# Decode attention on one core: all small PSUM tiles in one bank, a third V granule kept in PSUM

## The chip, the core and the metric

The kernel runs on one core of a Trainium2 chip. The metric is the device time in microseconds (us) of one execution; lower is better. TensorE is written PE, its weight loads PEld, VectorE DVE, ScalarE ACT, GpSimd POOL and SyncE SP, as in the profile.

## The reference

Two decoder layers with the same weights and the same caches run on eight rows (B) of one token each. D is 640, there are 32 heads of 128, 4096 cached positions, and a feed-forward width of 1728. All data are bf16.

```python
def A(x, k_cache, v_cache, wq, wo):      # x: (8, 1, 640)
    q = (x @ wq).reshape(B, Sq, 32, 128).transpose(0, 2, 1, 3)
    scores = einsum("bhqd,bhkd->bhqk", q, k) * 128 ** -0.5
    p = softmax(scores, axis=-1)
    o = einsum("bhqk,bhkd->bhqd", p, v)
    return o.transpose(0, 2, 1, 3).reshape(B, Sq, 4096) @ wo
def F(x, w1, w2):
    return relu(x @ w1) @ w2

x = x + A(layernorm(x));  x = x + F(layernorm(x))
x = x + A(layernorm(x));  x = x + F(layernorm(x))
```

Both layers read the same K and V caches, so what of a row's cache still lies on the chip when its second layer comes needs no second load.

## The kernel before, in words

**Tiles.** Heads go in pairs; a pair has one K tile and one V tile of 2 MB. Each tile is four granules of 512 KiB (128 partitions of 2048 bf16). An arena in SBUF has 26 slots (`G`) of one granule each. A *visit* is one head pair of one row in one layer: 16 pairs, 8 rows, 2 layers, so 256 visits.

**Order.** A planner in Python, `plan`, writes out the order of all work for all engines ahead of time, and nothing reorders it later. Row 0 runs its first layer. Then, for each row b, four visits of row b+1's first layer (`AHEAD`) stand before row b's second layer, so that the feed-forward steps of row b's first layer have time to finish. The second layer takes pairs 15, 14, 13 first, and then 0 to 12. K of visit i stands before V of visit i-1.

**What stays on the chip.** The granules that the second layer needs first are kept in the arena: 21 granules (`G - SPARE`), K of pairs 15, 14, 13, V of 15 and 14, and the first of V of pair 13. While they are kept, five slots rotate. The next `STASH` granules, of V of pair 13, are copied into PSUM when the first layer has used them (`stash`, L464 to L470, two VectorE copies each) and back into the arena for the second layer (`unstash`, L472 to L475, one copy on ScalarE and one on VectorE each). These granules are not loaded a second time. PSUM has eight banks; a stashed granule takes two.

**Loads.** SP issues every load (`do_load`, L478), in the planner's order, when the slots that it fills are free. The planner puts up to several neighbouring granules into one load (`LEADS`) where many slots are free; while granules are kept, loads are single.

**Steps of a visit**, with the lines of the profile:

- K granules (L524): 16 weight loads and matmuls each, scores into `s_ps`.
- `M1` (L530): VectorE takes the maximum of the scores per partition. `T` (L534): TensorE turns it into `blk_ps`. `M2` (L538, L540): VectorE takes the maximum over that. `B` (L543): TensorE broadcasts it into `blk_ps`. `E` (L547, L551): ScalarE reads it and takes two exponentials from `s_ps`.
- `L` (L556): TensorE sums the exponentials over partitions into `blk_ps`. `I` (L562, L566): VectorE reduces and inverts.
- V granules (L512): four matmuls each into `o_ps`. `OC` (L570): ScalarE copies the result out.
- `OG` (L575): TensorE gathers it into `oy_ps`. `O` (L585): VectorE reads that and scales it.
- First layer, and the last row's second layer: `W` (L592), TensorE, the output projection into `oy_ps`; `Y` (L601), VectorE, adds it to x.
- Second layer: `Q` (L496), TensorE, the query of a later pair into `blk_ps`; `QC` (L504), ScalarE, copies it out.

At a row's end in the first layer come the steps of `finish`: sums, `mean` (L355) and `var` (L369) by TensorE into `oy_ps` with VectorE reading each (L359, L390), an inverse square root on GpSimd (L391 to L401, L375), five `up` steps (L417) and a relu (L425, L428), five `down` steps (L434) and an `add` (L441), and then the same normalisation again for the second layer's queries. The planner deals these steps out between the granules, one or two after each.

**PSUM banks before:** `o_ps`, `s_ps`, `blk_ps` and `oy_ps` have one bank each, and four hold the two stashed granules. `s_ps` has two halves, for even and odd visits:

```python
s_tiles[i] = s_ps[:, i % 2]
```

Of the kernel before, what the change touches and what calls it, by code (L numbers as in the profile page):

```python
# [9 lines left out]
FP32 = mybir.dt.float32  # L10
BF16 = mybir.dt.bfloat16
ACT = mybir.ActivationFunctionType
ALU = mybir.AluOpType
# [4 lines left out]
GP = 4  # L18
G = 26
SPARE = 5  # L20
STASH = 2
LEADS = ((9, 8), (6, 4), (5, 2))
AHEAD = 4
BANK = 512
# [215 lines left out]
def kernel(  # L240
# [91 lines left out]
    arena = kv.tile([P, G * GW], BF16, name="arena")  # L332
    OR = 96 + CJ
    o_ps = ps.tile([P, CJ * Dh], FP32, name="o_ps")
    s_ps = ps.tile([P, 2, 2 * NJ], FP32, name="s_ps")
    blk_ps = ps.tile([P, BANK], FP32, name="blk_ps")
    oy_ps = ps.tile([P, BANK], FP32, name="oy_ps")
    stash_ps = [ps.tile([P, 2 * BANK], BF16, name=f"stash{n}_ps") for n in range(STASH * GW // (2 * BANK))]
    per = len(stash_ps) // STASH
    nc.vector.memset(o_ps, 0.0)  # L340

    up_parts = [range(f, min(f + 3, FC)) for f in range(0, FC, 3)]
    visits, ops = plan(B, NP, len(up_parts), DC)
    q1, s_tiles, P_tiles, m_tiles, o_tiles, blk, oy, invL, oT, nmax, st = ({} for _ in range(11))

    def ln_steps(b0, nb, xln, key):
        x = xT[:, b0 : b0 + nb, :]

        def sums():
            s1 = st[key, "s1"] = sm.tile([P, nb], FP32, name="s1", bufs=1)  # L350
            nc.vector.tensor_reduce(out=s1, in_=x, axis=AX.X, op=ALU.add)

        def mean():
            st[key, "mean"] = oy_ps[:, 64 : 64 + nb]
            nc.tensor.matmul(st[key, "mean"], lhsT=ones_f, rhs=st[key, "s1"], start=True, stop=True)  # L355

        def center():
            xc = st[key, "xc"] = sm.tile([P, nb, DC], FP32, name="xc", bufs=1)
            nc.vector.scalar_tensor_tensor(  # L359
                out=xc, in0=_free(st[key, "mean"], [(1, nb), (0, DC)]), scalar=-1.0 / D, in1=x, op0=ALU.mult, op1=ALU.add  # L360
            )
            sq = sm.tile([P, nb, DC], FP32, name="sq", bufs=1)
            nc.vector.tensor_tensor(out=sq, in0=xc, in1=xc, op=ALU.mult)
            s2 = st[key, "s2"] = sm.tile([P, nb], FP32, name="s2", bufs=1)
            nc.vector.tensor_reduce(out=s2, in_=sq, axis=AX.X, op=ALU.add)

        def var():
            st[key, "var"] = oy_ps[:, 72 : 72 + nb]
# [35 lines left out]
    def finish_steps(layer, b):  # L404


        b0, nb = (b, 1) if layer == 0 else (0, B)
        xf = sm.tile([P, nb, DC], BF16, name="xf", bufs=1)
        key = layer, b

        def up(k):
            if k == 0:
                st[key, "h"] = oy_ps[:, 128 : 128 + FC * nb].rearrange("p (f b) -> p f b", b=nb)
            for f in up_parts[k]:
                fs = f_sizes[f]
                for c in range(DC):
                    nc.tensor.matmul(  # L417
                        st[key, "h"][:fs, f, :], lhsT=w1_sb[:, c, f * P : f * P + fs], rhs=xf[:, :, c],
                        start=(c == 0), stop=(c == DC - 1),
                    )  # L420

        def relu():
            hT = st[key, "hT"] = sm.tile([P, FC, nb], BF16, name="hT", bufs=1)
            if n_full:
                nc.scalar.activation(out=hT[:, :n_full], in_=st[key, "h"][:, :n_full], func=ACT.Relu)  # L425
            if Dff % P:
                rem = Dff % P
                nc.scalar.activation(out=hT[:rem, n_full:], in_=st[key, "h"][:rem, n_full:], func=ACT.Relu)  # L428

        def down(c):  # L430
            if c == 0:
                st[key, "y"] = oy_ps[:, 256 : 256 + DC * nb].rearrange("p (c b) -> p c b", b=nb)
            for f, fs in enumerate(f_sizes):
                nc.tensor.matmul(  # L434
                    st[key, "y"][:, c, :], lhsT=w2_sb[:fs, f, c * P : (c + 1) * P],
                    rhs=st[key, "hT"][:fs, f, :], start=(f == 0), stop=(f == FC - 1),
                )
# [12 lines left out]
        return first, ln_steps(b, 1, xlns[b], (key, 2))  # L450
# [28 lines left out]

    def do_q0(g):  # L480

        q_ps = blk_ps[:, 256 : 256 + 2 * GP * B].rearrange("p (h b) -> p h b", b=B)
        for h in range(2 * GP):
            for c in range(DC):
                nc.tensor.matmul(
                    q_ps[:, h, :], lhsT=wq_sb[:, g, c, h * Dh : (h + 1) * Dh], rhs=xln0[:, :, c],
                    start=(c == 0), stop=(c == DC - 1),
                )
        nc.scalar.copy(out=q0[:, g * 2 * GP : (g + 1) * 2 * GP, :], in_=q_ps)

    def do_q(b, hp):
        q_ps = st["q", b, hp] = blk_ps[:, 320:322]
        g, n = divmod(hp, GP)
        for h in range(2):
            for c in range(DC):
                nc.tensor.matmul(  # L496
                    q_ps[:, h : h + 1], lhsT=wq_sb[:, g, c, (2 * n + h) * Dh : (2 * n + h + 1) * Dh],
                    rhs=xlns[b][:, 0, c : c + 1], start=(c == 0), stop=(c == DC - 1),
                )

    def take_q(b, hp):
        if b not in q1:
            q1[b] = sm.tile([P, H], BF16, name="q1", bufs=2)
        nc.scalar.copy(out=q1[b][:, 2 * hp : 2 * hp + 2], in_=st.pop(("q", b, hp)))  # L504

    def do_mm(which, i, g, u):
        layer, b, hp = visits[i]
# [22 lines left out]
        nc.vector.tensor_reduce(out=m_tiles[i], in_=s_tiles[i].rearrange("p (h j) -> p h j", h=2), axis=AX.X, op=ALU.max)  # L530

    def do_t(i):
        blk[i] = blk_ps[:, : P + 2 + 2 * NJ]
        nc.tensor.matmul(blk[i][:2, :P], lhsT=m_tiles.pop(i), rhs=ident, start=True, stop=True)  # L534

    def do_m2(i):
        hmx = sm.tile([2, 1], FP32, name="hmx")
        nc.vector.tensor_reduce(out=hmx, in_=blk[i][:2, :P], axis=AX.X, op=ALU.max)  # L538
        nmax[i] = sm.tile([2, 2], BF16, name="diag")
        nc.vector.tensor_tensor(out=nmax[i], in0=ident[:2, :2], in1=_free(hmx, [(0, 2)]), op=ALU.mult)  # L540

    def do_b(i):
        nc.tensor.matmul(blk[i][:, P : P + 2], lhsT=ones_b, rhs=nmax.pop(i), start=True, stop=True)  # L543

    def do_e(i):
        nm = sm.tile([P, 2], FP32, name="nmax")
        nc.scalar.activation(out=nm, in_=blk[i][:, P : P + 2], func=ACT.Copy, scale=-inv_sqrt_dh)  # L547
# [6 lines left out]

    def do_l(i):
        nc.tensor.matmul(  # L556
            blk[i][:, P + 2 :], lhsT=ones_p, rhs=P_tiles[i].rearrange("p h j -> p (h j)"), start=True, stop=True
        )

    def do_i(i):  # L560
        L = sm.tile([P, 2], FP32, name="lsum")
        nc.vector.tensor_reduce(  # L562
            out=L, in_=blk.pop(i)[:, P + 2 :].rearrange("p (h j) -> p h j", h=2), axis=AX.X, op=ALU.add
        )
        invL[i] = sm.tile([P, 2], FP32, name="invL", bufs=3)
        nc.vector.reciprocal(out=invL[i], in_=L)  # L566
# [3 lines left out]
        nc.scalar.copy(out=o_tiles[i][:OR], in_=o_ps[:OR, :].rearrange("p (j d) -> p j d", j=CJ))  # L570

    def do_og(i):
        oy[i] = oy_ps[:, : 2 + DC * B]
        for j in range(CJ):
            nc.tensor.matmul(  # L575
                oy[i][:, :2], lhsT=o_tiles[i][:OR, j, :], rhs=gsel[:OR, j, :], start=(j == 0), stop=(j == CJ - 1)
# [27 lines left out]
                L=do_l, I=do_i, OC=do_oc, OG=do_og, O=do_o, W=do_w, Y=do_y, C=do_finish, Q0=do_q0, Q=do_q, QC=take_q)  # L604

    with tc.manual_schedule(engines={ENG.PE, ENG.DVE, ENG.Activation, ENG.Pool, ENG.SP}):
        xT_ps = oy_ps[:, : B * DC]
        nc.tensor.matmul(xT_ps, lhsT=x_bf, rhs=ident[: B * DC, : B * DC], start=True, stop=True)
        nc.vector.tensor_copy(out=xT, in_=xT_ps.rearrange("p (b c) -> p b c", b=B))
        xln0 = consts.tile([P, B, DC], BF16, name="xln0")  # L610
# [1 line left out]
            step()  # L612
        for op in ops:
            does[op[0]](*op[1:])
        r_ps = oy_ps[: B * DC, :P]
# [56 lines left out]
```

## Time and profile before

| | |
|---|---|
| three runs | 2372.40, 2376.29, 2371.31 us; median 2372.4 us |
| the profiled execution's own time | 2376.09 us |
| its span in the profile | 2374.3 us |
| granted TensorE clock | 1.0 |
| bytes moved by DMA | 996.04 MB, 420 GB/s over the span |
| TensorE matmuls | 1292.5 us busy, 54% of the span |
| VectorE, ScalarE, GpSimd | 377.7, 355.9 and 42.8 us busy |

The page of the profile gives busy time for each engine; the span cut into 40 slices of 59 us with the DMA rate in each; the chain of work that ended last; groups of instructions by line; and the loads by size. A wait is written with the engine and line that ended it: "PE s_ps L524 <- DMA arena" means that a K matmul waited for a load. In rows in order of time, the first number is the start, the second the length, both in us; "x16" says that 16 instructions are merged; brackets hold the idle time before the first of them and what ended it. Matmuls overlap, and their ends are modelled, so the start of the next instruction tells more than the end of the last.

### The profile page before, as it was taken

How to read it: one execution, taken by the hardware profiler on the slowest of the kernel's cores; microseconds unless marked ns; L12 is line 12 of the kernel's file. 1: busy time of each engine (PE TensorE's matmuls, PEld its weight loads, DVE VectorE, ACT ScalarE, POOL GpSimd, SP SyncE). 2: the span in 40 equal slices, each digit the busy share in tenths (PEclk: the TensorE clock that was granted, in tenths of full speed). 3: DMA queues.
4: the chain of work that ended last, by engine and by line, in shares of the span. 5: the costliest groups of instructions: out<-in, count | busy, mean ns of one | idle time of the engine just before them, and what ended most of it. 6: DMA issues, size and time to landing. Idle time of an engine off the chain costs nothing.

```text
span 2374.3 us, 57948 instructions
## 1 busy us (share of the span) xinstructions
PE 1292.5 (54%) x26486; PEld 783.7 (33%) x26486; DVE 377.7 (16%) x1840; ACT 355.9 (15%) x1195; POOL 42.8 (2%) x198
## 2 busy tenths in 40 slices
PE   3436644476445754458454574446744466545845
PEld 2324322243223532225222352223422244223523
DVE  1102111121111211112111121112211112112211
ACT  1111211111111211112111121111211112111211
POOL 0000000000000000000000000000000000000000
DMA  9999999999999999999999999999999999999997
GB/s 411 428 429 403 428 432 431 429 398 433 428 433 427 391 433 428 433 423 404 430 434 433 406 401 431 433 431 408 420 431 430 430 408 417 431 432 410 405 434 302
DMA packets 92794, 996.04 MB, mean 420 GB/s; under 512 B 10372, under 2 KB 10372, under 8 KB 54916
## 3 DMA queue, kind: packets, MB, share of 16 engines
q1 hardware_dynamic: 92548, 992.33, 99.1%
q8 instruction: 207, 3.39, 0.5%
q14 instruction: 39, 0.32, 0.0%
HBM read 992.27 MB, written 0.01 MB: 418 GB/s over the span
## 4 chain that ended last, share of the span: by engine, by line
DMA 81%; PE 14%; DVE 2%; ACT 2%; issue 1%; POOL 1%; SPq 0%; POOLq 0%; DVEq 0%; ACTq 0%
DMA arena<-in_A_kv_dram 81%; PE o_ps L512 5%; PE s_ps L524 5%; ACT o_sb L570 1%; DVE hmx L538 1%; PE oy_ps L575 1%; PE blk_ps L496 1%; PE blk_ps L543 1%; DVE diag L540 0%; PE oy_ps L592 0%; PE blk_ps L534 0%; PE oy_ps L434 0%; DMA wq_sb<-in_A_wq_dram 0%; DVE arena L475 0%; POOL root L399 0%
## 5 line engine op out<-in xcount | busy, mean ns | idle before, releaser
L512 PE MATMUL o_ps<-arena,P_sb 128*4 128x512 bf16 x4096 | 564.8, 599 | 373.9 <-DMA arena<-in_A_kv_dram 371.6
L524 PEld LDWEIGHTS <-arena 128*128 128x128 bf16 x16384 | 501.6, 105 | 667.0 <-DMA arena<-in_A_kv_dram 660.7
L524 PE MATMUL s_ps<-q_96,arena 128*128 128x1 bf16 x8192 | 275.2, 166 | 371.9 <-DMA arena<-in_A_kv_dram 360.0
L547 ACT ACTIVATE nmax<-blk_ps 128x2 f32<-128x2 f32 x256 | 44.0, 172 | 1638.3 <-PE blk_ps L543 1638.3
L512 PEld LDWEIGHTS <-P_sb 128*4 128x4 bf16 x4096 | 90.6, 81 | 442.5 <-issue 429.4
L570 ACT CAST o_sb<-o_ps 100x512 bf16<-100x512 f32 x256 | 149.8, 585 | 228.8 <-PE o_ps L512 228.8
L562 DVE TENSOR_REDUCE lsum<-blk_ps 128x2 f32<-128x64 f32 x256 | 57.3, 224 | 588.6 <-PE blk_ps L556 588.6
L530 DVE TENSOR_REDUCE mrow<-s_ps 128x2 bf16<-128x64 f32 x256 | 57.5, 224 | 578.1 <-PE s_ps L524 542.6
L551 ACT ACTIVATE P_sb<-s_ps,nmax 128x32 bf16<-128x32 f32 x512 | 118.8, 283 | 8.2
L538 DVE TENSOR_REDUCE hmx<-blk_ps 2x1 f32<-2x128 f32 x256 | 71.4, 279 | 207.2 <-PE blk_ps L534 207.2
L556 PEld LDWEIGHTS <-onesb_c 128*128 128x128 bf16 x256 | 26.4, 103 | 199.7 <-issue 199.7
L585 DVE TENSOR_TENSOR oT<-oy_ps,invL 128x2 bf16<-128x2 f32 x128 | 20.4, 160 | 350.5 <-PE oy_ps L575 350.5
L575 PE MATMUL oy_ps<-gsel,o_sb 100*128 100x2 bf16 x1024 | 66.1, 168 | 17.5 <-ACT o_sb L570 0.7
L534 PE MATMUL blk_ps<-ident,mrow 128*2 128x128 bf16 x256 | 70.0, 274 | 3.1 <-DVE mrow L530 3.1
L543 PEld LDWEIGHTS <-onesb_c 2*128 2x128 bf16 x256 | 25.1, 98 | 125.1 <-issue 125.0
L556 PE MATMUL blk_ps<-P_sb,onesb_c 128*128 128x64 bf16 x256 | 59.7, 233 | 0.0
L575 PEld LDWEIGHTS <-o_sb 100*128 100x128 bf16 x1024 | 47.4, 106 | 33.6 <-ACT o_sb L570 29.6
L524 PE MATMUL s_ps<-q_22833,arena 128*128 128x1 bf16 x1024 | 34.1, 166 | 43.6 <-DMA arena<-in_A_kv_dram 43.4
L524 PE MATMUL s_ps<-q_18821,arena 128*128 128x1 bf16 x1024 | 33.9, 166 | 43.4 <-DMA arena<-in_A_kv_dram 43.3
L524 PE MATMUL s_ps<-q_2773,arena 128*128 128x1 bf16 x1024 | 33.9, 166 | 42.7 <-DMA arena<-in_A_kv_dram 42.7
L524 PE MATMUL s_ps<-q_14809,arena 128*128 128x1 bf16 x1024 | 34.1, 166 | 42.4 <-DMA arena<-in_A_kv_dram 41.9
L524 PE MATMUL s_ps<-q_10797,arena 128*128 128x1 bf16 x1024 | 33.9, 166 | 42.6 <-DMA arena<-in_A_kv_dram 42.5
(179 smaller groups left out, 781.2 us busy)
## 6 DMA issues: line engine op xcount, KB each, us to landing
arena<-in_A_kv_dram SPq DMA_DIRECT2D x109, 4096.0 KB, 24.8
arena<-in_A_kv_dram SPq DMA_DIRECT2D x100, 2048.0 KB, 25.2
arena<-in_A_kv_dram SPq DMA_DIRECT2D x348, 512.0 KB, 6.2
arena<-in_A_kv_dram SPq DMA_DIRECT2D x16, 2560.0 KB, 22.6
arena<-in_A_kv_dram SPq DMA_DIRECT2D x35, 1024.0 KB, 12.8
arena<-in_A_kv_dram SPq DMA_DIRECT2D x17, 1536.0 KB, 24.4
arena<-in_A_kv_dram SPq DMA_DIRECT2D x6, 3072.0 KB, 23.3
wq_sb<-in_A_wq_dram SPq DMA_DIRECT2D x4, 1280.0 KB, 30.0
```

Source lines behind the costliest of these rows:

```text
L512: nc.tensor.matmul(o_ps[32 * c : 32 * c + CJ, :], lhsT=P_tiles[i][:, h, j : j + CJ], rhs=arena[:, at + c * CJ * Dh : at + (c + 1) * CJ * D ...
L524: nc.tensor.matmul(s_tiles[i][:, j : j + 1], lhsT=arena[:, at + n * P : at + (n + 1) * P], rhs=q, start=True, stop=True)
L530: nc.vector.tensor_reduce(out=m_tiles[i], in_=s_tiles[i].rearrange("p (h j) -> p h j", h=2), axis=AX.X, op=ALU.max)
L534: nc.tensor.matmul(blk[i][:2, :P], lhsT=m_tiles.pop(i), rhs=ident, start=True, stop=True)
L538: nc.vector.tensor_reduce(out=hmx, in_=blk[i][:2, :P], axis=AX.X, op=ALU.max)
L543: nc.tensor.matmul(blk[i][:, P : P + 2], lhsT=ones_b, rhs=nmax.pop(i), start=True, stop=True)
L547: nc.scalar.activation(out=nm, in_=blk[i][:, P : P + 2], func=ACT.Copy, scale=-inv_sqrt_dh)
L551: nc.scalar.activation(out=P_tiles[i][:, h, :], in_=S[:, h, :], func=ACT.Exp, bias=nm[:, h : h + 1], scale=inv_sqrt_dh)
L556: nc.tensor.matmul(blk[i][:, P + 2 :], lhsT=ones_p, rhs=P_tiles[i].rearrange("p h j -> p (h j)"), start=True, stop=True)
L562: nc.vector.tensor_reduce(out=L, in_=blk.pop(i)[:, P + 2 :].rearrange("p (h j) -> p h j", h=2), axis=AX.X, op=ALU.add)
L570: nc.scalar.copy(out=o_tiles[i][:OR], in_=o_ps[:OR, :].rearrange("p (j d) -> p j d", j=CJ))
L575: nc.tensor.matmul(oy[i][:, :2], lhsT=o_tiles[i][:OR, j, :], rhs=gsel[:OR, j, :], start=(j == 0), stop=(j == CJ - 1))
```

## The change

The three tiles `s_ps`, `blk_ps` and `oy_ps` become one tile of one bank, `small_ps`; each former tile is now a range of its columns. Up to 320 columns hold the steps of a visit and the two normalisation sums, and the last 192 hold the feed-forward results, the first layer's queries of row 0 and the two transposes at the start and the end. That leaves six banks, and `STASH` goes from 2 to 3: the second, third and fourth granules of V of pair 13 are all stashed. The steps, their shapes and the engines that run them stay as they were.

```diff
-STASH = 2
+STASH = 3
...
-    s_ps = ps.tile([P, 2, 2 * NJ], FP32, name="s_ps")
-    blk_ps = ps.tile([P, BANK], FP32, name="blk_ps")
-    oy_ps = ps.tile([P, BANK], FP32, name="oy_ps")
+    small_ps = ps.tile([P, BANK], FP32, name="small_ps")
+    s_ps = small_ps[:, : 4 * NJ].rearrange("p (i j) -> p i j", i=2)
+    turn_ps, max_ps, q_ps = small_ps[:2, 128:256], small_ps[:, 256:258], small_ps[:, 258:260]
+    sum_ps = small_ps[:, 128 : 128 + 2 * NJ]
+    oy_ps = small_ps[:, 260 : 262 + DC * B]
+    ln_ps = small_ps[:, 304:320]
+    ffn_ps = small_ps[:, 320:512]
...
-            st[key, "mean"] = oy_ps[:, 64 : 64 + nb]
+            st[key, "mean"] = ln_ps[:, :nb]
...
-            st[key, "var"] = oy_ps[:, 72 : 72 + nb]
+            st[key, "var"] = ln_ps[:, 8 : 8 + nb]
...
-                st[key, "h"] = oy_ps[:, 128 : 128 + FC * nb].rearrange("p (f b) -> p f b", b=nb)
+                st[key, "h"] = ffn_ps[:, : FC * nb].rearrange("p (f b) -> p f b", b=nb)
...
-                st[key, "y"] = oy_ps[:, 256 : 256 + DC * nb].rearrange("p (c b) -> p c b", b=nb)
+                st[key, "y"] = ffn_ps[:, FC * B : FC * B + DC * nb].rearrange("p (c b) -> p c b", b=nb)
...
-        nc.tensor.matmul(blk[i][:2, :P], lhsT=m_tiles.pop(i), rhs=ident, start=True, stop=True)
+        nc.tensor.matmul(turn_ps, lhsT=m_tiles.pop(i), rhs=ident, start=True, stop=True)
...
-        nc.vector.tensor_reduce(out=hmx, in_=blk[i][:2, :P], axis=AX.X, op=ALU.max)
+        nc.vector.tensor_reduce(out=hmx, in_=turn_ps, axis=AX.X, op=ALU.max)
...
-        nc.tensor.matmul(blk[i][:, P : P + 2], lhsT=ones_b, rhs=nmax.pop(i), start=True, stop=True)
+        nc.tensor.matmul(max_ps, lhsT=ones_b, rhs=nmax.pop(i), start=True, stop=True)
...
-            blk[i][:, P + 2 :], lhsT=ones_p, rhs=P_tiles[i].rearrange("p h j -> p (h j)"), start=True, stop=True
+            sum_ps, lhsT=ones_p, rhs=P_tiles[i].rearrange("p h j -> p (h j)"), start=True, stop=True
...
-        oy[i] = oy_ps[:, : 2 + DC * B]
+        oy[i] = oy_ps
```

The query products (`Q`, `Q0`) and the transposes at both ends are renamed in the same way.

More of the change, by code (lines that the diff above doesn't have):

```diff
@@ L343 @@
     visits, ops = plan(B, NP, len(up_parts), DC)
-    q1, s_tiles, P_tiles, m_tiles, o_tiles, blk, oy, invL, oT, nmax, st = ({} for _ in range(11))
+    q1, s_tiles, P_tiles, m_tiles, o_tiles, oy, invL, oT, nmax, st = ({} for _ in range(10))
     def ln_steps(b0, nb, xln, key):
@@ L480, in do_q0 @@
     def do_q0(g):
-        q_ps = blk_ps[:, 256 : 256 + 2 * GP * B].rearrange("p (h b) -> p h b", b=B)
+        q_ps = ffn_ps[:, : 2 * GP * B].rearrange("p (h b) -> p h b", b=B)
         for h in range(2 * GP):
@@ L491, in do_q @@
     def do_q(b, hp):
-        q_ps = st["q", b, hp] = blk_ps[:, 320:322]
         g, n = divmod(hp, GP)
@@ L503, in take_q @@
             q1[b] = sm.tile([P, H], BF16, name="q1", bufs=2)
-        nc.scalar.copy(out=q1[b][:, 2 * hp : 2 * hp + 2], in_=st.pop(("q", b, hp)))
+        nc.scalar.copy(out=q1[b][:, 2 * hp : 2 * hp + 2], in_=q_ps)
     def do_mm(which, i, g, u):
@@ L532, in do_t @@
     def do_t(i):
-        blk[i] = blk_ps[:, : P + 2 + 2 * NJ]
-        nc.tensor.matmul(blk[i][:2, :P], lhsT=m_tiles.pop(i), rhs=ident, start=True, stop=True)
+        nc.tensor.matmul(turn_ps, lhsT=m_tiles.pop(i), rhs=ident, start=True, stop=True)
     def do_m2(i):
         hmx = sm.tile([2, 1], FP32, name="hmx")
-        nc.vector.tensor_reduce(out=hmx, in_=blk[i][:2, :P], axis=AX.X, op=ALU.max)
+        nc.vector.tensor_reduce(out=hmx, in_=turn_ps, axis=AX.X, op=ALU.max)
         nmax[i] = sm.tile([2, 2], BF16, name="diag")
@@ L542, in do_b @@
     def do_b(i):
-        nc.tensor.matmul(blk[i][:, P : P + 2], lhsT=ones_b, rhs=nmax.pop(i), start=True, stop=True)
+        nc.tensor.matmul(max_ps, lhsT=ones_b, rhs=nmax.pop(i), start=True, stop=True)
     def do_e(i):
         nm = sm.tile([P, 2], FP32, name="nmax")
-        nc.scalar.activation(out=nm, in_=blk[i][:, P : P + 2], func=ACT.Copy, scale=-inv_sqrt_dh)
+        nc.scalar.activation(out=nm, in_=max_ps, func=ACT.Copy, scale=-inv_sqrt_dh)
         P_tiles[i] = sm.tile([P, 2, NJ], BF16, name="P_sb", bufs=3)
@@ L562, in do_i @@
         nc.vector.tensor_reduce(
-            out=L, in_=blk.pop(i)[:, P + 2 :].rearrange("p (h j) -> p h j", h=2), axis=AX.X, op=ALU.add
+            out=L, in_=sum_ps.rearrange("p (h j) -> p h j", h=2), axis=AX.X, op=ALU.add
         )
@@ L606 @@
     with tc.manual_schedule(engines={ENG.PE, ENG.DVE, ENG.Activation, ENG.Pool, ENG.SP}):
-        xT_ps = oy_ps[:, : B * DC]
+        xT_ps = ffn_ps[:, : B * DC]
         nc.tensor.matmul(xT_ps, lhsT=x_bf, rhs=ident[: B * DC, : B * DC], start=True, stop=True)
@@ L614 @@
             does[op[0]](*op[1:])
-        r_ps = oy_ps[: B * DC, :P]
+        r_ps = ffn_ps[: B * DC, :P]
         nc.tensor.matmul(r_ps, lhsT=outT.rearrange("p b c -> p (b c)"), rhs=ident, start=True, stop=True)
```

## The prediction

> **What bounds the kernel now.** I read the page first, then stretches of the run by their DMA rate, then who waits for whom, then the order of time in one stretch. The page has the DMA engines busy in nearly every slice, and the chain that ended last runs through them:
>
> ```profile
> DMA  9999999999999999999999999999999999999997
> GB/s 411 428 429 403 428 432 431 429 398 433 428 433 427 391 433 428 433 423 404 430 434 433 406 401 431 433 431 408 420 431 430 430 408 417 431 432 410 405 434 302
> DMA 81%; PE 14%; DVE 2%; ACT 2%; issue 1%; POOL 1%; SPq 0%; POOLq 0%; DVEq 0%; ACTq 0%
> ```
>
> So bytes set the time, but the rate dips about every fifth slice, eight times in all: once a row. Stretches (us; the last two columns are DMA share and GB/s) show both kinds of time:
>
> ```profile
> 540.00:770.00 230.00, 112.87 (x2366) 66.22 (x2363) 33.48 (x162) 31.45 (x108) 0.00 (x0) 1.00 1.00 430
> 483.80:526.30 42.50, 31.43 (x644) 22.35 (x644) 7.66 (x43) 5.90 (x23) 5.26 (x24) 1.00 1.00 393
> 1353.20:1396.50 43.30, 31.16 (x630) 22.10 (x630) 7.72 (x43) 5.90 (x22) 5.26 (x24) 1.00 0.99 370
> ```
>
> In plain time TensorE (first number after the length) is busy half the time at 430 GB/s. In the dip, 21 of the 26 arena slots hold kept granules, five rotate, loads go out singly as TensorE frees a slot, and TensorE is busy three quarters of the time, because the feed-forward steps of the row before fall there. I call these 42 us the narrow window. Next, TensorE's waits (total us, times, longest):
>
> ```profile
> PE s_ps L524 <- DMA arena<-in_A_kv_dram: 625.2, 199, 7.6
> PE o_ps L512 <- DMA arena<-in_A_kv_dram: 371.6, 159, 13.0
> PE s_ps L524 <- ACT P_sb L551: 8.1, 9, 2.0
> PE oy_ps L434 <- DVE oT L585: 2.2, 7, 0.3
> ```
>
> Two lessons. TensorE has 997 us of waiting on loads, a wide cover. And lines three and four show the price of a shared bank: the K matmuls write one half of s_ps, the exponentials read the other half; `down` writes oy_ps from column 256, `O` reads columns 0 and 1. No data joins them, yet TensorE waits. So the program waits by bank, not by column. The order of time in a narrow window shows one such wait, and a place that is still free of it:
>
> ```profile
> 495.13 0.46 ACT L551 ACTIVATE P_sb<-s_ps,nmax 128x32 bf16<-128x32 f32 x2
> 495.65 0.57 PE L524 MATMUL s_ps<-q_96,arena 128*128 128x1 bf16 x16 [0.76 <-ACT P_sb L551]
> 497.51 0.21 PE L556 MATMUL blk_ps<-P_sb,onesb_c 128*128 128x64 bf16 x1
> 497.54 0.56 PE L417 MATMUL oy_ps<-xf,w_sb 128*128 128x1 bf16 x15
> 497.76 0.22 DVE L530 TENSOR_REDUCE mrow<-s_ps 128x2 bf16<-128x64 f32 x1 [3.53 <-PE blk_ps L556]
> 497.90 0.21 DVE L562 TENSOR_REDUCE lsum<-blk_ps 128x2 f32<-128x64 f32 x1
> ```
>
> `L` (L556) and `up` (L417) start while VectorE still reads s_ps and then blk_ps. In one bank neither may.
>
> **The bytes.** A granule is 128 x 2048 bf16, 512 KiB. One load less per row, eight rows: at 430 GB/s 1.22 us each, 9.8 us less. The other side of the stash is cheap: two more VectorE copies at 0.686 us (L466) per row fall at 474 to 478, where TensorE waits 4.2 us for a load; one ScalarE copy at 1.015 us and one VectorE copy at 0.686 us (L475) come back after the window, ahead of `E`, which costs TensorE some 0.1 us in a stretch where slots come free faster than loads can fill them. Without that cover it would be 1.0 us per row. I take nothing.
>
> **The waits.** Each small product is read right after it is written, and now the next write into the bank waits for that read. From the rows: a read starts 0.04 us after the matmul's end, takes 0.16 (`O`, `Y`, `QC`), 0.22 (`M1`, `I`), 0.28 (`M2`) or 0.66 us (`E`, three instructions), and a write follows 0.06 us later. Against today's issue that is 0.5 us behind `L`, 0.4 behind `OG`, 0.4 behind `W` or `Q`: 1.3 us per visit, 333 us over 256 visits. V matmuls write o_ps and aren't held, so `T`/`M2` and `B`/`E` cost nothing where a V granule follows them.
>
> In plain time this is hidden. A visit takes TensorE 4.8 us when nothing is late (540.44 less 535.62 between two `OG`), so 6.1 us; its eight granules take the DMA 8 x 1.22 = 9.8 us. Loads stay queued.
>
> In the narrow window it isn't. I follow row 1 to row 2 step by step, moving each write into the bank behind the last read, and give each start's delay against the trace. `var` (492.23) waits for `M1`, the next K granule for the read of `var`: +0.71. The exponentials, which held K before, leave +0.63, `up` 0 behind GpSimd +0.58. `L` (497.51) waits for `M1`: +1.10. `up` 1 waits for `I`: +1.62. `up` 2 (498.66) waits for `M2`: +2.07. `up` 3 (499.82) waits for `E`: +2.90. Two load gaps give back 0.22. `down` 0 (502.35) waits for `I`: +3.19. K (505.48) waits for `Y`: +3.38. `down` 3 (507.16) waits for `M1`: +3.65. A load gap gives back 0.84; `down` 4 (509.22) waits for `M2`: +3.25; `mean` (510.48) for `E`: +4.08. A gap of 1.06 at 514.48 brings +3.34 and one of 0.53 at 515.70 +3.07, but `Q` (516.59) sits behind GpSimd's chain that started 4.08 late; `W` behind `QC` +4.47, K behind `Y` +4.86, K behind `QC` (518.16) +4.92. The four V granules that follow had load gaps of 0.63, 0.55, 0.54 and 0.60, so the lag out of the window is 2.8 us.
>
> What counts is the queue. The load that goes out when that last K granule is done left at 518.77; it will leave at 523.7. Today it lands some 5.5 us later (K granules land 1.24 us apart: 523.06 + 1.24 = 524.3), because four others are ahead. With TensorE 4.9 us late these have landed, and the load has the engines to itself. How fast is it then? The trace shows no lone 512 KiB load; its nearest row is the first one of the run:
>
> ```profile
> 0.72 0.41 SPq L284 DMA_DIRECT2D x_bf<-in_A_x_dram  x1
> 2.42 0.10 PEld L608 LDWEIGHTS <-x_bf 40*128 40x128 bf16 x1 [2.42 <-DMA x_bf<-in_A_x_dram]
> arena<-in_A_kv_dram SPq DMA_DIRECT2D x348, 512.0 KB, 6.2
> ```
>
> 10 KB take 1.70 us; with 1.22 us of transfer my estimate is 2.9 us. It lands at 526.7 and not 524.3: 2.4 us of DMA time lost per window. Bounds: transfer alone, 1.2 us, loses 0.6; the loaded latency of 5.5 us loses the whole 4.9. Below nothing it can't be, since the waits only add. I take 2.4, as the 1.70 us row is the only one with no queue ahead. The eighth window holds row 6's second-layer visits beside the same feed-forward steps; I give it the same. 8 x 2.4 = 19.2 us.
>
> The Trainium skill has this cost too: DMA: Bandwidth & Descriptors, section Anatomy of one DMA, gives a fixed part of about 2.0 us and a rate of 436 GB/s. By that the lone load takes 3.2 us, an estimate, 2.7 us per window and 21.6 in all; it was fitted on another issue path, and the 1.70 us row decides here. A rule against the change stands in PSUM — Partial Sum Buffer, section PSUM bank collisions raise a hardware error: guard by bank and quadrant, not by address. Lines three and four of the waits show the bank; freeing other quadrants would change nothing in the sum, as nearly all these tiles span all partitions.
>
> **The tail.** After the last K tile the same three waits and `M1` push `T` back by 0.6 us, and the last V granules wait behind it: +0.6. The rest of the tail is one chain already.
>
> **Sum.** 19.2 - 9.8 + 0.6 = +10.0 us. The profiled execution took 2376.1 us (span 2374.3), so 2386.1 by its own time; the median of the three runs is 3.7 us below it: 2382.4.
>
> **Rivals.**
> *The waits are hidden (faster).* TensorE's 997 us of load waits swallow all of it, in the window too: -9.8 + 0.6, 2363. For it: the DMA share in the window is 1.00, so a queue seems to stand behind the loads. Against: with five slots and 1.25 us per load the cycle is 6.25 us, of which 5.5 are the load itself; a lag of 4.9 us eats nearly all that could stand in a queue. It decides if the window's lag stays under some 2.6 us (5.5 less 2.9). This is also where it would go if the program waited by column. 0.16.
>
> *A cheap floor.* A lone load needs only its transfer: 8 x 0.6 - 9.2 = -4.4, 2368. Against: no load of the trace is that quick. 0.10.
>
> *The window breaks (slower still).* The latency does not shrink with the queue, and each window pays 4.9: 39.2 - 9.2 = +30, 2402 or more. For it: the fifth window already runs at 370 GB/s with the same work, so this state is fragile. It decides if loads issued late still take over 5 us to land. 0.16.
>
> **How the numbers follow.** Forecast, with a loss of 1.6 to 3.6 us per window (2376 to 2392): 0.58. The range, 2366 to 2406, is the sum's bounds (-4.4 and +30, so 2368 and 2402) with a little on either side; it leaves out the hidden case and little else. About 0.2%, 4.7 us, is what a measurement of this kernel can tell from no change. Slower by more: 0.52 of the forecast and the broken window, 0.68. Faster by more: the hidden case and a share of the cheap floor, 0.18. Within: the rest, 0.14.
>
> **What would show it.** Eight loads of 512 KB fewer than the 348 of now, or as many bytes less if loads are grouped anew. TensorE's waits: K matmuls on VectorE (`I`, `O`, `Y`) and ScalarE (`QC`) in the hundreds of us, load waits down by about as much. `up` and `down` held by `I`, `M2` and `E`. In the narrow windows a rate some 20 GB/s lower and 2 to 3 us more length; 430 GB/s in plain time as now. Wrong if the windows keep their length (hidden), if plain time falls below 425 GB/s, or if K matmuls show no new waits.

## The result

The changed kernel took 2406.99 us (median of four runs, 2404.1 to 2412.6) and the kernel before 2374.35 beside it (2371.3 to 2376.6): a ratio of 1.0141, 95% interval 1.0118 to 1.0164. It is slower, as forecast, but by 33 us and not by 10; the time stands 1 us above the range. Below, "over" and "under" are the ratio less one times 2372.4 us, against the kernel before on the same chip.

### The profile page after: what moved, and what is told of

The parts are those of the page before. It is cut to its first block, busy times and chain, and to the rows that moved or that the text cites. A ratio compares the mean times of both kernels' runs of the same rounds, so it can differ in the third digit from the quotient of the medians.

```text
span 2405.3 us, 57936 instructions
## 1 busy us (share of the span) xinstructions
PE 1348.9 (56%) x26486; PEld 819.7 (34%) x26486; DVE 392.9 (16%) x1864; ACT 362.6 (15%) x1203; POOL 42.8 (2%) x198
## 4 chain that ended last, share of the span: by engine, by line
DMA 66%; PE 23%; DVE 4%; issue 3%; ACT 2%; POOL 2%; DVEq 0%; SPq 0%; POOLq 0%; ACTq 0%
DMA arena<-in_A_kv_dram 66%; PE small_ps L527 9%; PE o_ps L515 7%; PE small_ps L499 1%; DVE hmx L540 1%; PE small_ps L421 1%; DVE lsum L564 1%; PE small_ps L438 1%; PE small_ps L594 1%; PE small_ps L558 1%; ACT arena L479 1%; PE small_ps L545 1%; PE small_ps L577 1%; POOL root L403 1%; ACT P_sb L553 0%
## 5 line engine op out<-in xcount | busy, mean ns | idle before, releaser
L527 PEld LDWEIGHTS <-arena 128*128 128x128 bf16 x16384 | 538.4, 104 | 549.3 <-DMA arena<-in_A_kv_dram 348.0
L527 PE MATMUL small_ps<-q_96,arena 128*128 128x1 bf16 x8192 | 275.7, 165 | 340.6 <-DMA arena<-in_A_kv_dram 256.5
L564 DVE TENSOR_REDUCE lsum<-small_ps 128x2 f32<-128x64 f32 x256 | 57.5, 225 | 579.4 <-PE small_ps L558 579.4
L533 DVE TENSOR_REDUCE mrow<-small_ps 128x2 bf16<-128x64 f32 x256 | 57.5, 224 | 455.3 <-PE small_ps L527 455.3
L540 DVE TENSOR_REDUCE hmx<-small_ps 2x1 f32<-2x128 f32 x256 | 71.2, 278 | 317.0 <-PE small_ps L536 317.0
L553 ACT ACTIVATE P_sb<-small_ps,nmax 128x32 bf16<-128x32 f32 x512 | 119.3, 284 | 8.2
L536 PE MATMUL small_ps<-ident,mrow 128*2 128x128 bf16 x256 | 74.8, 292 | 3.1 <-DVE mrow L533 3.1
L499 PEld LDWEIGHTS <-wq_sb 128*128 128x128 bf16 x1280 | 53.3, 104 | 45.5 <-issue 45.0
L577 PE MATMUL small_ps<-gsel,o_sb 100*128 100x2 bf16 x1024 | 62.9, 165 | 0.7 <-ACT o_sb L572 0.7
L558 PE MATMUL small_ps<-P_sb,onesb_c 128*128 128x64 bf16 x256 | 59.6, 233 | 5.6 <-DVE mrow L533 3.5
L527 PE MATMUL small_ps<-q_14833,arena 128*128 128x1 bf16 x1024 | 32.8, 165 | 36.6 <-DMA arena<-in_A_kv_dram 27.3
L594 PE MATMUL small_ps<-oT,wo_sb 128*128 128x1 bf16 x1280 | 52.0, 165 | 1.7 <-ACT q_6796 L507 0.2
```

The lines of the kernel that those rows point to most:

```text
L499: nc.tensor.matmul(q_ps[:, h : h + 1], lhsT=wq_sb[:, g, c, (2 * n + h) * Dh : (2 * n + h + 1) * Dh], rhs=xlns[b][:, 0, c : c + 1], start=( ...
L527: nc.tensor.matmul(s_tiles[i][:, j : j + 1], lhsT=arena[:, at + n * P : at + (n + 1) * P], rhs=q, start=True, stop=True)
L536: nc.tensor.matmul(turn_ps, lhsT=m_tiles.pop(i), rhs=ident, start=True, stop=True)
L540: nc.vector.tensor_reduce(out=hmx, in_=turn_ps, axis=AX.X, op=ALU.max)
L553: nc.scalar.activation(out=P_tiles[i][:, h, :], in_=S[:, h, :], func=ACT.Exp, bias=nm[:, h : h + 1], scale=inv_sqrt_dh)
L558: nc.tensor.matmul(sum_ps, lhsT=ones_p, rhs=P_tiles[i].rearrange("p h j -> p (h j)"), start=True, stop=True)
```

## The profile after

The page: DMA rate in the 40 slices, the chain that ended last, and the single loads.

```profile
GB/s 411 429 429 367 427 429 430 428 364 430 429 433 426 362 434 428 433 415 373 432 430 433 406 373 431 430 430 402 389 431 431 428 390 407 428 431 403 381 431 299
DMA 66%; PE 23%; DVE 4%; issue 3%; ACT 2%; POOL 2%; DVEq 0%; SPq 0%; POOLq 0%; ACTq 0%
DMA packets 97258, 991.84 MB, mean 412 GB/s; under 512 B 10868, under 2 KB 10868, under 8 KB 57332
arena<-in_A_kv_dram SPq DMA_DIRECT2D x363, 512.0 KB, 6.1
```

The slices between the dips are as before; the dips, 391 to 408 before, fell to between 362 and 390. TensorE's part of the chain went from 14 to 23%. 4.20 MB fewer are moved, the eight granules; but there are more single loads, 363 for 348, since the planner grouped them anew. (In the last row, 363 is the number of loads and 6.1 their median time in us from issue to landing.)

Stretches at the same places of the program as those shown of before (plain time, the second and the fifth narrow window; length, PE, PEld, DVE, ACT and POOL busy, clock, DMA share, GB/s):

```profile
550.00:780.00 230.00, 121.71 (x2393) 70.77 (x2386) 35.70 (x168) 32.37 (x111) 0.00 (x0) 1.00 1.01 430
488.80:534.60 45.80, 31.30 (x608) 21.85 (x609) 7.61 (x42) 5.88 (x22) 5.26 (x24) 1.00 0.96 348
1368.60:1415.40 46.80, 30.87 (x594) 21.45 (x595) 7.75 (x42) 6.01 (x22) 5.26 (x24) 1.00 0.96 353
```

Plain time keeps its 430 GB/s. The windows are 3.3 and 3.5 us longer (42.50 and 43.30 before) and fall from 393 and 370 GB/s to 348 and 353. TensorE's waits:

```profile
PE o_ps L515 <- DMA arena<-in_A_kv_dram: 442.5, 142, 12.1
PE small_ps L527 <- DMA arena<-in_A_kv_dram: 326.5, 109, 7.8
PE small_ps L527 <- DVE lsum L564: 51.7, 164, 0.3
PE small_ps L527 <- DVE xT L603: 34.7, 127, 0.4
...
PE small_ps L527 <- DVE oT L587: 22.2, 88, 0.3
```

K matmuls (now L527) wait for VectorE's reads of `L`, `W` and `OG` (`I`, `Y`, `O`), with which they share no data; the waits for loads fell from 997 to 769 us. In order of time, the place in the second window that was free of such waits:

```profile
503.21 0.22 DVE L533 TENSOR_REDUCE mrow<-small_ps 128x2 bf16<-128x64 f32 x1 [3.42 <-PE small_ps L527]
503.48 0.21 PE L558 MATMUL small_ps<-P_sb,onesb_c 128*128 128x64 bf16 x1 [0.38 <-DVE mrow L533]
503.73 0.23 DVE L564 TENSOR_REDUCE lsum<-small_ps 128x2 f32<-128x64 f32 x1 [0.30 <-PE small_ps L558]
...
504.01 0.54 PE L421 MATMUL small_ps<-xf,w_sb 128*128 128x1 bf16 x15 [0.32 <-DVE lsum L564]
...
507.49 0.54 PE L421 MATMUL small_ps<-xf,w_sb 128*128 128x1 bf16 x15 [0.76 <-ACT P_sb L553]
```

`L` waits for `M1`, `up` 1 for `I`, `up` 3 for `E`, as the prediction stepped it. The rate at which the window's loads arrive, in slices of 1 us from 490 to 530, first the kernel before, then after:

```profile
GB/s 324 340 369 385 385 381 406 385 410 381 393 430 406 426 422 414 430 389 430 418 410 410 410 414 410 401 418 377 406 369 393 418 373 385 430 369 426 377 410 418
```

```profile
GB/s 414 422 307 234 246 365 307 324 381 397 397 311 410 369 365 410 369 352 250 299 340 328 250 258 340 385 389 365 393 426 414 397 356 356 324 303 352 385 287 344
```

There is no gap of silence before one lone load; the whole window runs thin. The loads of this stretch in the kernel after, with their median time to landing:

```profile
DMA packets 3806, 13.92 MB, mean 348 GB/s; under 512 B 424, under 2 KB 424, under 8 KB 3800
arena<-in_A_kv_dram SPq DMA_DIRECT2D x26, 512.0 KB, 5.7
```

A load takes about as long as before: cut at the same steps, as below, the second window has 27 loads with a median of 5.7 us in either kernel. They are spread over 39.7 us for 36.3. With the mean of the recorded times (6.0 us before, 5.7 after) that makes 4.4 loads in flight before and 3.9 after, an estimate.

**Where the 31 us of span went** (2405.3 less 2374.3). I cut the span at the same steps in both: a window runs from the start of the last V granule of a row's first layer to the start of the last V granule of the next row's third visit. The seven windows average 39.75 us for 36.57 (+3.18 each, 22.3 together); the six stretches between them 253.86 for 253.27 (+3.5 together); what follows the last window, with the eighth feed-forward and the tail, 407.0 for 401.3 (+5.7); the first begins 0.6 earlier. The sum is 30.9, and what is left is rounding. Such lengths come from one profiled execution of each kernel, and a few tenths of a us per window or stretch tell nothing: the kernel before and its variant with another order, whose times can't be told apart below, differ by 0.3.

## The experiments

The theory after the result: late TensorE in the narrow window, through the bank's waits, and loads issued late that are not as quick as estimated. The rivals: the waits in plain time, the new grouping of the loads, the bank's waits as such rather than the lateness.

**One half of the change each.** The bank without the third granule (on the kernel after):

```diff
-STASH = 3
+STASH = 2
```

> The shared bank alone: two granules stashed as before, so the loads and the order of work are those of the kernel before. Theory late loads: the bank's waits are the whole loss and the third granule brings back 8 to 10 us, so this is slower than the changed kernel: 2410 to 2416 us, 37 to 42 over before. Rival third granule (its copies, one slot filled without a load, and loads grouped anew cost as much as the load saves): 2398 to 2404 us, some 26 over before, from the narrow windows alone.

Measured 2411.28, ratio 1.0161 (1.0146 to 1.0176): 38 over, as the theory had it. Windows 40.17, between them 254.32.

The third granule without the bank (on the kernel before; the third is copied into the first one's place, so this kernel doesn't keep all the values of V):

```diff
-STASH = 2
+STASH = 3
...
-        for n, t in enumerate(stash_ps[slot * per : (slot + 1) * per]):
+        for n, t in enumerate(stash_ps[slot % 2 * per : (slot % 2 + 1) * per]):
```

> The third granule alone: three tiles of their own bank as before, the planner of the changed kernel, eight loads fewer. The third granule is copied into the PSUM tiles of the first, so the values of two granules of V are wrong while every copy and load is made. Theory late loads: 8 to 10 us faster than before, 2363 to 2367 us. Rival third granule: within 3 us of before, or slower.

Measured 2365.98, 0.9969 (0.9956 to 0.9982): 7.4 under. Between the windows 252.25, which is 1.0 less per row; windows 36.07. The two halves add up, 38 - 7 = 31 for the change's 33, so they can be studied apart. The granule's worth was nearly as forecast (9.8, inside the interval of 4.3 to 10.4); the bank's price was not.

**The grouping of the loads** (on the kernel after: planned as with two granules, and the third one's load then replaced by its copy):

```diff
-    stash = first[G - SPARE : G - SPARE + STASH]
+    stash = first[G - SPARE : G - SPARE + 2]
...
+                op = ("unstash", 2, op[4])
```

> The changed kernel with the loads grouped as before: the planner runs for two granules, and afterwards the third granule's copy out and copy back are put where its planner has them, the second one in place of its load. 340 single loads and the same larger ones as before, in place of 363 single ones and fewer of 4 MB. It tells whether the new groups cost. Theory late loads: plain time is bound by bytes in either grouping, within 3 us of the changed kernel: 2403 to 2409 us. Rival groups: the smaller loads cost the part that the catch-up stretch lost, 2396 to 2402 us.

Measured 2405.21, 1.0137 (1.0114 to 1.0161): no difference from the kernel after. This kernel has 340 single loads for 363, so the new grouping costs nothing that can be told here.

**Which waits.** Feed-forward and normalisation in a bank of their own, all steps of a visit in the other, two granules stashed (on the kernel after):

```diff
-STASH = 3
+STASH = 2
...
-    ln_ps = small_ps[:, 304:320]
-    ffn_ps = small_ps[:, 320:512]
+    wide_ps = ps.tile([P, BANK], FP32, name="wide_ps")
+    ln_ps = wide_ps[:, 304:320]
+    ffn_ps = wide_ps[:, 320:512]
```

> Two small banks and two stashed granules: the visit's tiles share one bank, the feed-forward and normalisation results have another. Loads as before. Theory late loads: the lag in the narrow window came from the feed-forward steps held behind M1, I, M2 and E and the other way round; without it TensorE is late by 1 us or less and the time is 4 to 12 us over before. Rival visit waits (the 1.3 us of waits in each of 256 visits is what costs, wherever it falls): as slow as the single bank with two granules, 26 to 42 us over before.

Measured 2387.27, 1.0057 (1.0042 to 1.0071): 13.5 over, a little more than the 4 to 12 expected. The windows are back at 36.53, so the coupling of feed-forward and visits makes their length, and without it some 25 us (38 - 13.5) of the bank's price are gone. But what lies between them went up to 254.84, 1.57 per row. That is the part that the prediction called hidden.

**Lateness without any shared bank** (on the kernel before; the first layer's `up` and `down` run their matmuls twice, with the same result):

```diff
-                for c in range(DC):
+                for c in list(range(DC)) * (2 if layer == 0 else 1):
...
-            for f, fs in enumerate(f_sizes):
+            for f, fs in list(enumerate(f_sizes)) * (2 if layer == 0 else 1):
```

> The kernel before with its own banks, but every up and down matmul of the first layer's feed-forward is made twice (the second chain starts afresh, so the values stay): ten times some 0.45 us more TensorE time in each narrow window, no wait added. It tells lateness from the bank. Theory late loads: TensorE is late by about 4 us in the window without any shared bank, and that starves the loads just the same: 3 to 4 us in each of eight windows, 2395 to 2408 us. Rival bank (a shared bank slows the matmuls or reads themselves): nothing to see, 2370 to 2378 us.

Measured 2400.02, 1.0114 (1.009 to 1.0138): 27 over; windows 39.45, between them 253.11 (before: 253.27), after the last one 406.35. An `up` step took 0.96 us for 0.56 and a `down` step 1.15 for 0.60, so each window holds 4.7 us more TensorE work. The page's rate shows the same dips as the changed kernel, with the banks as before:

```profile
GB/s 410 432 428 380 428 432 433 426 377 432 429 433 426 378 433 427 435 418 387 431 432 432 410 395 432 430 431 402 403 431 430 429 390 416 429 433 397 382 432 304
```

So lateness in the window is enough to lengthen it; in the changed kernel the bank is what makes TensorE late. Is there slack first, as the prediction had it (2.6 us)? With `up` alone doubled (the first of the two edits):

> The kernel before, banks and stash as before; only the five up steps of each first layer run their matmuls twice (same result). From the run with up and down doubled, an up step takes 0.40 us more (0.96 for 0.56) and a down step 0.55, so this kernel makes TensorE 2.0 us late in each of the 8 narrow windows where that one made it 4.7 us late and cost 28.7 us. Theory A (each us of lateness costs about the same, because the latency of a load hardly falls with the queue): 28.7 x 2.0 / 4.7 = 12, 8 to 16 over the kernel before. Theory B (the prediction's slack: the queue has some 2.6 us to spare, and only lateness beyond it costs): 0 to 4 over.

Measured 2383.2, 1.0044 (1.003 to 1.0058): 10.4 over; windows 38.00. Some 2.0 us of added work lengthen a window by 1.43 us and 4.7 us by 2.88, 0.6 to 0.7 for each us, so no 2.6 us come free. Net of the load gaps that give some of it back, TensorE is 1.6 and 2.4 us late in these two kernels at the window's last K granule (mean of seven windows), and 4.1 in the changed kernel, whose windows grew by 3.18. That a smaller lateness costs too isn't shown: with the feed-forward apart TensorE is 1.3 us late at that granule, and the windows keep their length.

**How fast is a late load?** A kernel by itself: single 512 KiB loads into 1 to 8 rotating slots, 40 for each count, and 16 matmuls as a granule's use:

```python
for k in range(N):
    o = (k % slots) * GW
    for n in range(GJ):
        nc.tensor.matmul(s_ps[:, 0, n : n + 1], lhsT=arena[:, o + n * P : o + (n + 1) * P], rhs=ident[:, :1], start=True, stop=True)
    if k + slots < N:
        load(k + slots)
```

> The attention is left out. Loads of one 512 KiB granule, 40 for each count of rotating slots from 1 to 8, each used by 16 K matmuls (0.6 us) before its slot is loaded again. It measures what the prediction estimated at 2.9 us: a granule load with no other ahead of it. Forecast's term (1.70 + 1.22 us): the period with one slot is 2.9 + 0.6 = 3.5 us, and with three slots the loads run at the full rate, 1.22 us apart. Theory late loads: a load takes 4.6 to 5.6 us even when few are ahead, as in the trace after; so 5 to 5.5 us per granule with one slot, 2.6 with two, 1.75 with three, 1.35 with four, and 1.25 only from five on.

Stretches with 1, 2, 3, 4, 5, 6, 7 and 8 slots (length, PE, PEld, DVE, POOL busy, clock, DMA share, GB/s):

```profile
4.90:166.00 161.10, 22.88 (x624) 19.69 (x624) 0.00 (x0) 0.00 (x0) 1.00 0.39 127
170.00:266.00 96.00, 23.42 (x640) 20.18 (x640) 0.00 (x0) 0.00 (x0) 1.00 0.67 218
268.00:342.00 74.00, 22.88 (x630) 19.69 (x628) 0.00 (x0) 0.00 (x0) 1.00 0.82 275
346.00:406.00 60.00, 23.19 (x636) 20.00 (x637) 0.00 (x0) 0.00 (x0) 1.00 0.96 348
407.00:460.00 53.00, 22.79 (x624) 19.60 (x624) 0.00 (x0) 0.00 (x0) 1.00 1.01 387
461.00:512.00 51.00, 22.92 (x624) 19.73 (x624) 0.00 (x0) 0.00 (x0) 1.00 1.02 403
513.00:566.00 53.00, 23.23 (x638) 20.04 (x639) 0.00 (x0) 0.00 (x0) 1.00 1.03 402
567.00:618.00 51.00, 22.73 (x624) 19.53 (x623) 0.00 (x0) 0.00 (x0) 1.00 0.98 387
```

From issue to landing with 1, 2, 3, 4 and 5 slots: 3.43, 4.27, 4.73, 5.45 and 5.84 us (medians). With one slot a granule takes 4.1 us (512 KiB at 127 GB/s), between the two expectations. Two readings. A lone load takes 3.43 us (the quickest 3.32), not 2.9. And five slots, the number that rotates in the window, are barely enough for the engines: six bring 403 GB/s for 387, four only 348. A slot that waits for a late TensorE is one slot fewer.

**One slot more.** `SPARE` from 5 to 6 keeps 20 granules and rotates six slots, at the price of one more load per row. The edit is the same on both kernels:

```diff
-SPARE = 5
+SPARE = 6
```

On the kernel after:

> The changed kernel with SPARE 6 instead of 5: 20 granules kept, 3 stashed, so the bytes of the kernel before, and six slots rotate in the narrow window. With six slots the run on slots alone had 1.28 us per granule against 1.33 with five, and a load more in hand when TensorE is late. Theory late loads: most of the window's loss goes, 2 to 3 us less per window than the changed kernel, against 1.2 us per row of bytes: 2390 to 2402 us, still over before. Rival (the waits cost wherever they fall): the bytes are added and nothing comes back, 2412 to 2420 us.

Measured 2398.36, 1.0109 (1.008 to 1.0139): 26 over, 7.6 better than the kernel after. Windows 37.28 for 39.75.

On the kernel before:

> The kernel before with SPARE 6 instead of 5: 20 granules kept, 2 stashed, eight loads more than before, and six slots in the narrow window. Theory late loads: the dip to 393 GB/s in the narrow window comes from five slots being too few for the loads' latency of 5.5 us; with six the window gains about 2 us and the row pays 1.2 us of bytes: 2364 to 2372 us. Rival (the dip has another cause, such as the feed-forward steps): 2380 to 2386 us, the bytes alone.

Measured 2373.3, 1.0004 (0.9992 to 1.0015), just above the theory's range and well below the rival's. Windows 35.25 for 36.57 (1.3 gained), between them 254.38 for 253.27 (1.1 lost to the extra load): even without the shared bank a sixth slot was worth about as much as a kept granule.

**Taking waits out.** The scores in a bank of their own, the rest in one, two granules stashed (on the kernel after):

```diff
-STASH = 3
+STASH = 2
...
-    s_ps = small_ps[:, : 4 * NJ].rearrange("p (i j) -> p i j", i=2)
+    s_ps = ps.tile([P, 2, 2 * NJ], FP32, name="s_ps")
```

> Two small banks and two stashed granules, cut in another way than the run with the feed-forward apart: the scores s_ps keep a bank of their own, all other small tiles share one. K matmuls then wait for none of I, O, Y, QC, and the exponentials hold nothing; up and down still wait for I, M2 and the first of E's reads. Loads as before. Theory late loads: TensorE is late by 1.5 us in the window, which is below what starves the loads (a lag of 1 us did not lengthen it, 4.4 us lengthened it by 2.9), and nothing is late where TensorE catches up: 3 to 9 us over before. Rival (two small banks cost the same however they are cut): 12 to 15 us over before, as with the feed-forward apart.

Measured 2388.05, 1.0071 (1.0053 to 1.0089): 16.8 over, more than either expected. K matmuls no longer wait for VectorE, but windows are 38.06, since the feed-forward still shares its bank with `L`, `T` and `B`:

```profile
PE small_ps L421 <- DVE lsum L564: 3.8, 8, 0.7
...
PE small_ps L421 <- DVE hmx L540: 3.0, 8, 0.4
```

Eight times each: once per window, the eighth feed-forward's included. On top of this, half a third granule in the bank that is left (two halves of PSUM, 256 KiB loaded instead of 512):

```diff
-STASH = 2
+STASH = 3
...
+                if p == 2:
...
+                    ops.append(("half", visits[i][1], tile_at(NP, which, visits[i][2]) * UNIT + g, u))
...
+    stash_ps = [ps.tile([P, 2 * BANK], BF16, name=f"stash{n}_ps") for n in range(5)]
```

> The same two small banks leave five banks for the stash, so two and a half granules stay: of the third granule one half comes back from PSUM by ScalarE and the other half is loaded, 256 KB in place of 512 KB. A version meant to beat both kernels. Theory late loads: 3 to 9 us of waits less 4 us of bytes: 2 us under to 5 us over before. Rival (a half load costs as much as a whole one, since a load takes over 3 us anyway): as the run without it.

Measured 2382.3, 1.0035 (1.0021 to 1.0048): 8.3 over, 8.5 less than without it and more than the theory's 5.

Then the order. The planner's step takes the cheapest chain first, so a short product is often followed at once by a feed-forward step that must wait for its read. Turned round, the feed-forward goes first and the products last, and their reads run beside the V granule that follows:

```diff
+        n, now = 0, []
...
-                take(c)
+                now.append(c)
+        for c in now[::-1]:
+            take(c)
```

On the kernel after:

> The changed kernel with another order inside a step: of the chains that are due, the feed-forward matmuls go out first and the short products with their reads last, so that M2, I and E are read while a V granule, which isn't held, runs. No data or load changes. Theory late loads: some 2 us of the 4 us lag in the window go, and 1.5 to 2.5 us per window: 12 to 20 us less than the changed kernel, 2386 to 2395 us. Rival (order inside a step does not matter, the next K granule waits instead): 2402 to 2409 us.

Measured 2394.36, 1.0092 (1.0075 to 1.011): 12 better than the kernel after; windows 38.28 for 39.75.

On the half granule's kernel:

> Two and a half stashed granules with the scores in a bank of their own, and the order of the run before: reads last. The version with the fewest waits and five banks of stash. Theory late loads: the lag in the window falls under 1 us and the bytes count: 2 to 8 us under before. Rival (half loads cost as whole ones): 0 to 5 us over before.

Measured 2368.31, 0.9985 (0.9973 to 0.9996): 3.6 under the kernel before: the only kernel here that does all its work and whose whole interval lies under the kernel before, though by less than the 0.2% that a measurement can tell at ease.

On the kernel before, to see if the order is better in itself:

> The kernel before, banks and stash as before; only the order within a step is turned: the costliest chain first, the short products that are read at once last. Theory A (the order helped the one-bank kernels, by 12 us each time, because reads then run beside the next granule and no write stands right behind them): with separate banks there is nothing to save, within 4 us of the kernel before. Theory B (the order is better in itself, for the feed-forward starts earlier in each window): 6 to 14 us under the kernel before, and the kernel with two and a half granules and this order owes its 3.6 us to the order and not to the third granule.

Measured 2369.52, 0.9994 (0.9985 to 1.0003): no difference that can be told. The order acts on the bank's waits.

On the scores-apart kernel with two granules:

> Scores in a bank of their own, all other small tiles in one, two granules stashed, and the costliest chain first within a step. With the old order this layout was 16.8 us over the kernel before. Theory A (waits for the bank carry that, and the order takes out most of them): 3 to 8 over. Theory B (the order does the same 12 us for any layout, as it did in two): also 3 to 8, but then the kernel before with this order must be some 12 us under; read together with that run. Against both: over 12, the order would only help where half a granule more is stashed.

Measured 2372.6, 1.0001 (0.999 to 1.0012). It takes out all of that layout's 16.8 us, more than either expected (3 to 8 over); windows 36.51 for 38.06, between them 253.06. Two banks for the small tiles instead of three are thus free, given this order. How much of the 3.6 us is the half granule's stays open, as the intervals of these three runs overlap.

## Why the prediction was right and wrong

The forecast was +10.0 us; the span grew by 31.0. On the cuts above, with the forecast in brackets: seven windows +22.3 (16.8), the six stretches between them +3.5 (-7.3, the bytes), the end +5.7 (+0.6), the beginning -0.6 (0). So of the 21 us that the sum lacks, some 11 lie in plain time, 5.5 in the windows and 5 at the end.

**Right: waits by bank, and their order.** Measured against the kernel before, in the second window, with the forecast in brackets: `L` 1.01 us later (1.10), `up` 1 1.51 (1.62), `up` 2 1.92 (2.07), `up` 3 2.71 (2.90), `down` 0 2.84 (3.19), `down` 3 3.00 (3.65), `mean` 3.57 (4.08), the last K granule 4.10 (4.92). The bank rule, drawn from two lines of waits, held at each step, and the lag was 0.8 too high at the end. The rival "hidden", waits by column included, falls. Each of these banks holds a single tile, so no run here tells a wait by bank from a wait by tile.

**Wrong: the load that goes out late.** This is the step whose mechanism failed. It said that four others have landed by then, so the load has the engines to itself and takes 2.9 us for some 5.5. That very load was issued at 518.77 and landed at 525.52 in the kernel before (6.75 us, where the prediction read 5.5), and at 527.82 and 533.45 in the kernel after (5.63). The second kernel is 4.97 us later at the window's start, so the load left 4.08 us late and gave back 1.12: it landed 2.96 us late, and the window grew by 3.2 on average, not by 2.4 (2.3 by the prediction's own terms, 523.7 + 2.9 - 524.3). The least that a load of this window took, of those whose landing is recorded, was 4.60 us (issued at 526.74). The forecast pictured one long stop. The lateness comes in many small steps, so load after load is issued somewhat late: when this one left, two or three others were still under way, for they had been held up too (three of them left at 522.50, 524.26 and 526.74). The median load stays at 5.7 us, and by the estimate above 3.9 instead of 4.4 are in flight. In the slots' run five slots bring 387 GB/s and four 348; the window fell from 393 to 348, as if one of its five slots were gone. Even the lone load was under-sized: 3.43 us by the slots' run. There the Trainium skill's DMA: Bandwidth & Descriptors, section Anatomy of one DMA, was nearer than the 1.70 us row: its fixed 2.0 us and 436 GB/s make 3.2 us, an estimate. Neither figure would have saved the sum, since no load was alone. The rival of a cheap floor falls too, as even a lone load took at least 3.32 us.

The slack of 2.6 us (5.5 less 2.9) falls with it, by the run with `up` doubled. The rival "the window breaks" came nearest to the mechanism: late loads still took 5.7 us in the median and 4.60 at the least. Its price per window, 4.9, was too high, but its total of 2402 is near, by luck: another term was missing.

**Wrong: plain time at nothing.** In us this step missed the most: the stretch between windows, forecast 1.22 shorter by the bytes, came out 0.59 longer. The DMA had 9.8 us of work per visit for TensorE's 6.1, and the 430 GB/s did stay. Yet with the feed-forward apart the visits' waits cost 1.57 us per row outside the windows, and in the bank alone 1.05. The first visits of the second layer are where the cover is missing: they use kept granules, and TensorE hardly waits for a load. TensorE's waits there, 529.8 to 549 before and 540 to 563 after:

```profile
PE o_ps L512 <- DMA arena<-in_A_kv_dram: 0.2, 1, 0.2
```

```profile
PE small_ps L527 <- DVE lsum L564: 1.3, 4, 0.3
PE small_ps L527 <- ACT q_6796 L507: 1.0, 4, 0.2
PE small_ps L499 <- DVE o_97 L587: 0.8, 3, 0.3
```

A visit takes TensorE 4.8 us there before (the last V granules start at 534.28, 539.10 and 543.92) and 5.8 after (545.36, 551.15 and 556.96), so there each visit pays 1.0 us of waits (the prediction had 1.3, hidden). By the fifth visit behind a window TensorE has fallen 6.0 us further behind (mean of six windows); the loads that follow give most of it back. With the scores in a bank of their own, where the K matmuls wait for none of these reads, it is 1.9 us, and the stretch is as long as before (253.31). Why 0.6 to 1.6 us per row stay of the 6 is not settled.

**The gain** was about right: 7.4 us measured (4.3 to 10.4) for 9.8.

**The end.** 0.6 for the tail and 2.4 for the eighth window were forecast, less two granules' loads (those of the last two rows); +5.7 was measured. Doubled matmuls alone, with no shared bank, give +5.0 there, and the feed-forward apart still gives +2.0, so most of it is probably the eighth feed-forward's lateness and not the tail's bank waits.

**Loads.** "Eight fewer single loads" was wrong, and "as many bytes less" right.

## What to carry to other kernels

Before you let lateness vanish in a queue, count the buffers that rotate against the number in flight that full rate needs; if these are nearly equal, as here, most of the lateness is paid. A latency measured under load does not shrink to the unloaded one because the consumer is late: measure rate and latency against the number of slots in one small run. Look for stretches that run on data already on the chip: there a DMA-bound kernel has no cover for TensorE's waits. If tiles must share a PSUM bank, keep apart those that are written beside each other's reads, and put the product that is read at once last, just ahead of work on another bank: here that turned 16.8 us of cost into none that can be told.

## What was not expected of the hardware

A DMA share near 1.00 is no sign of full rate: four slots show 0.96 at 348 GB/s, five 1.01 at 387, and the kernel's plain time 1.01 at 430. The kernel before had 1.00 at 393 in its window, which the prediction gave as the point for its hidden rival, a queue behind the loads. More than six slots brought nothing (403, 402 and 387 GB/s), while a load's time went on rising, from 7.00 us with six to 9.87 with eight.
